# Hash-bucketed attention kernel: one flag matmul per block, one normalisation per head, V's scale matmul ahead of the scores, bits in two steps

## Chip, core and metric

The kernel runs on one core of a Trainium2 chip. The metric is the device time of one execution in microseconds (us); three executions of the kernel before took 687.52, 689.46 and 691.98 us, so its time is 689.46 us (median). A core has a matrix engine (TensorE, PE; its weight loads are listed apart as PEld), VectorE (DVE), ScalarE (ACT), GpSimd (POOL) and a queue engine (SP) that issues most of the DMAs here.

## What is computed

Attention in which a query sees only the keys of its own hash bucket, then two dense layers. Shapes: batch 2, 8 heads, 768 positions, head size 64.

```python
q_bits = (einsum('bhsd,dk->bhsk', q, proj) > 0)          # 6 bits, k_bits the same way
mask = q_bucket[:, :, :, None] == k_bucket[:, :, None, :]
scores = where(mask, (1 / sqrt(D)) * q @ k.T, -1e9)
scores = scores - max(scores, axis=-1)
attn = exp(scores); attn = attn / (sum(attn) + 1e-9)
x = attn @ v                                              # then to (1536, 512)
h = maximum(maximum(x @ w1, x @ w2), x @ w3); x = h @ w_out
h = x @ w_in; return (h * clip(h + 3, 0, 6) / 6) @ w_out2
```

A query whose bucket holds no key has all scores at -1e9 and so gets the mean row of V.

## The kernel before

**Steps.** The 16 heads (8 pairs `p`, two heads `j` each; `h = 2p + j`) are cut into 96 score units, six for each head: two halves `hf` of 384 queries, three units of 256 keys each. A loop runs over steps `s` = 0 to 101 (`NST + LAG`). Step `s` writes out, in this order on TensorE: the block product `pv` of block `s - 6` (`LAG` is 6), the step's tasks, `scores` of unit `s`, and the row maxima `max_unit` of a later head (10 units ahead). Every engine runs its instructions in the order in which this loop writes them. The instructions that split an exponential (`psplit`) follow, then the tasks that are named in `AFTER` or come before step 8, and then the late tasks.

**One step on TensorE.** `scores` makes four matmuls of 384 columns (line 664): two of Q by K in high and low parts (`QB`, `KB`), two over rows of `T` tiles that hold the high parts, the hash bits and the row maxima. ScalarE reads the result `s` twice: exponential `E` in fp32 (line 668), and `ph`, the same in fp16 (line 671, one unit in twelve on VectorE). GpSimd subtracts (`pl`, line 686). `max_unit` makes two matmuls (line 614), which VectorE reduces (line 618). `pv` handles one block of 128 queries, three to a half, once all three units of that half are there: 6 key tiles times three matmuls of 65 columns (lines 698 to 700: `ph` by V's high and low half, `pl` by the high half; column 65 sums the weights), then two matmuls for the queries without a key: `FL` (one row of flags) by V's mean row in `VM`, its high half (line 703) and its low half (line 704). Each of these twenty loads its own weights.

**PSUM.** There are three pools: `s`, 2 buffers of two banks; `x`, one bank; `m`, three banks (maxima, bits, transposes, V's mean and scale). The three blocks of a half add into one `x` tile at columns 0, 66 and 132. `norm` (lines 710, 715, 718, on VectorE) reads it at the end of the half: denominator `xd`, reciprocal `xr`, product `xo`. As there is one `x` buffer, the first block of the next half waits for `xo`. It is written in steps with `s % 6` of 2 and 5, right behind the block.

**Other work that the change touches.** `vsum` (line 543) is one matmul with `ones` that spreads the pair's maximum of |V|, from which V's scale is made; it is named in `AFTER` and so is written behind the maxima of its step (`s % 12 == 6`). `bits` computes hash signs of a half pair: six matmuls (line 147) and one compare on VectorE (line 513); both halves stand in one step (`BT`, 13 steps ahead of the pair). `max_out` sends the two maximum rows (`T<-mr`) and the flags (`FL<-mf`, line 651) by DMA on SP's queue, two steps ahead of the head. `vmean` (line 596) sums V by matmuls whose result is the same on every partition, and makes `VM` from partition 0.

**After the loop** come the two dense layers: matmuls of 384 and 512 columns with three products each.

Of the kernel before, what the change touches and what calls it, by code (L numbers as in the profile page):

```python
# [24 lines left out]
VW = 130  # L25
# [7 lines left out]
RAMP = 8  # L33
AFTER = ("vmean", "vsum")
WARM = (9, 4, 3, 1)
# [18 lines left out]
AK, AQ = -15, -16  # L54
BT = (-13, -13)
BO = (-12, -11)
# [48 lines left out]
def body(ctx, tc, qT, kT, vP, projT, wts, consts, out):  # L105
# [251 lines left out]
    def attention():  # L357
# [5 lines left out]
        VV = [ap.tile([128, KT, 2, VW], F16, name=f"VV{i}") for i in range(2)]  # L363
        VM = [ap.tile([128, 2, VW], F16, name=f"VM{i}") for i in range(2)]
        FL = [ap.tile([128, S], F16, name=f"FL{i}") for i in range(3)]
# [224 lines left out]
        def vmean(p):  # L590
            u = unit()
            w = VV[p % 2]
            o = u[:, 0:130].rearrange("p (j d) -> p j d", j=2)
            for kt in range(KT):
                for c in (0, 65):
                    pe.matmul(
                        o, one16, w[:, kt, :, c:c + 65], start=kt + c == 0,
                        stop=kt == KT - 1 and c > 0,
                    )
            m = ap.tile([1, 2, 64], F32, name="vm_m")  # L600
            act.activation(out=m, in_=o[0:1, :, 0:64], func=AF.Copy, scale=1.0 / S)
            vm = VM[p % 2][0:1]
            eng = pool if p else dve
            eng.tensor_copy(out=vm[:, :, 0:64], in_=m)
            eng.tensor_tensor(out=vm[:, :, 65:129], in0=m, in1=vm[:, :, 0:64], op=ALU.subtract)

# [39 lines left out]
        def max_out(h, q=None, eng=None):  # L646
            r, g = st.pop(("mr", h, q))
            c = slice(0, S) if q is None else hsl(q)
            for i in range(2):
                copy(QA[h % NA][96 + i:97 + i, c], r[:, i, :], eng)  # L650
            (eng or sp).dma_start(out=FL[h % 3][0:1, c], in_=g)

# [36 lines left out]
        def pv(h, hf, q):  # L689
            p, j = divmod(h, 2)  # L690
            if q == 0:
                st["X", h, hf] = unit("x")
            o = st["X", h, hf][:, 66 * q:66 * q + 65]
            for kt in range(KT):
# [6 lines left out]
            c = slice(hf * HF + 128 * q, hf * HF + 128 * q + 128)  # L701
            f, vm = FL[h % 3][:, c], VM[p % 2][:, j, :]
            pe.matmul(o, f, vm[:, 0:65], start=False, stop=False)
            pe.matmul(o, f, vm[:, 65:130], start=False, stop=True)

        def norm(h, hf):
            p, j = divmod(h, 2)
            X = st.pop(("X", h, hf))[:, 0:198].rearrange("p (b d) -> p b d", b=3)
            d = a2.tile([128, 3], F32, name="xd")
            dve.tensor_scalar(  # L710
                out=d, in0=X[:, :, 64], scalar1=1e-9, scalar2=up[:, p:p + 1],
                op0=ALU.add, op1=ALU.mult,
            )
            r = a2.tile([128, 3], F32, name="xr")
            dve.reciprocal(out=r, in_=d)
            if j == 0 and hf == 0:
                st["xo", p] = a2.tile([128, 6, 128], F32, name="xo")
            dve.tensor_tensor(  # L718
                out=st["xo", p][:, 3 * hf:3 * hf + 3, 64 * j:64 * j + 64], in0=X[:, :, 0:64],
                in1=r.unsqueeze(2).to_broadcast([128, 3, 64]), op=ALU.mult,  # L720
            )
# [9 lines left out]
        def at(s, fn, *a):  # L731
            tasks.setdefault(s, []).append((fn, a))
# [54 lines left out]
        for p in range(NP):  # L787
# [36 lines left out]
            for j in range(2):  # L824
                h = 2 * p + j
                if h:
                    at(s0 + 6 * j + MF, max_fin, h)
                    at(s0 + 6 * j + MO, max_out, h)
                for hf in range(2):
                    at(s0 + 6 * j + 3 * hf + 2 + LAG, norm, h, hf)  # L830
            for hf in range(2):
# [24 lines left out]
        for s in range(NST + LAG):  # L856
            if 0 <= s - LAG < NST:
                pv(*idx(s - LAG))
# [9 lines left out]
            for g in gs:  # L868
                next(g, None)
            if 0 <= s - 1 < NST:  # L870
                psplit(*idx(s - 1), gs)
# [794 lines left out]
```

## Time and profile before

| | |
|---|---|
| three executions | 687.52, 689.46, 691.98 us |
| profiled execution | 693.22 us, of it span 691.4 us |
| PE busy | 668.5 us (97%) |
| PEld busy | 613.1 us (89%) |
| DVE, ACT, POOL busy | 507.7 (73%), 432.1 (63%), 330.8 (48%) us |
| mean granted clock of TensorE | 0.993 |

The attention loop fills the span up to about 250 us. A busy PE is not a full one: the profile lets each matmul last until its result is out, about 0.19 us for 65 columns, while the next starts 0.03 us later. What a matmul costs in a row of others is the distance from its start to the next one's start. A wait is idle time of an engine that a named instruction ended. The granted clock is 1.00 at TensorE's upper level (2.4 GHz) and 0.5 at its lower (1.2 GHz).

### The profile page before, as it was taken

Reading aid. Unit: us, or ns where it says so; the run is one execution under the profiler, and the core shown is the slowest. Engines: PE = TensorE matmul, PEld = TensorE weight load, DVE = VectorE, ACT = ScalarE, POOL = GpSimd, SP = SyncE. Lnnn points to the kernel's source line nnn. Section 1 sums busy time; section 2 is a strip of 40 time slices with the busy share of each in tenths; the row PEclk is TensorE's granted clock in tenths of the full one; section 3 lists DMA queues with packets and bytes.
Section 4 is the critical chain, followed back from the end, with each engine's and each line's share of the span. In section 5 each row is a group of like instructions: output and inputs, shape, how many; then the busy total and the mean of one; then the engine's idle time right before and its main releaser. Section 6 shows DMA issues by size and latency. Waiting matters only on the chain. (4 is left out here: it accounts for less than half of the span.)

```text
span 691.4 us, 13485 instructions
## 1 busy us (share of the span) xinstructions
PE 668.5 (97%) x5189; PEld 613.1 (89%) x5189; DVE 507.7 (73%) x978; ACT 432.1 (63%) x749; POOL 330.8 (48%) x280
## 2 busy tenths in 40 slices
PE   8999999999999999999999999899999999999998
PEld 7789898888898989999998899878898898898986
DVE  6888987999985547677667347974768687877664
ACT  7658787898888525574745456686656565665530
POOL 6778888899988240655441242313142331313100
PEclk9999999999999999999999999999999999999999
DMA  6655656667441000211121320022213030211004
GB/s 190 169 155 133 168 140 156 173 165 195 107 97 63 2 1 32 90 64 62 62 92 34 120 92 31 31 74 79 86 36 122 21 102 31 92 60 63 1 0 183
DMA packets 22527, 61.80 MB, mean 89 GB/s; under 512 B 3864, under 2 KB 4952, under 8 KB 22464
## 3 DMA queue, kind: packets, MB, share of 16 engines
q1 hardware_dynamic: 22032, 60.55, 30.7%
q8 instruction: 41, 0.67, 0.4%
q10 hardware_dynamic: 432, 0.40, 0.2%
q14 instruction: 22, 0.18, 0.1%
HBM read 38.87 MB, written 3.15 MB: 61 GB/s over the span
## 5 line engine op out<-in xcount | busy, mean ns | idle before, releaser
L686 POOL TENSOR_TENSOR pl<-E,ph 128x768 f16<-128x768 f32 x85 | 152.5, 1809 | 30.8 <-ACT ph L671 18.1
L618 DVE TENSOR_REDUCE mx<-m 128x1 f32<-128x384 f32 x192 | 96.7, 546 | 13.9 <-PE m L614 13.0
L668 ACT ACTIVATE E<-s 128x768 f32<-128x768 f32 x96 | 78.0, 813 | 40.7 <-PE s L664 32.9
L671 ACT ACTIVATE ph<-s 128x768 f16<-128x768 f32 x85 | 68.9, 811 | 0.0
L698 PEld LDWEIGHTS <-ph 128*128 128x128 f16 x576 | 54.3, 98 | 16.5 <-issue 10.5
L698 PE MATMUL x<-VV,ph 128*128 128x65 f16 x576 | 65.2, 196 | 2.7 <-DVE xo L718 1.9
L699 PE MATMUL x<-VV,ph 128*128 128x65 f16 x576 | 64.7, 197 | 0.0
L700 PE MATMUL x<-VV,pl 128*128 128x65 f16 x576 | 64.2, 194 | 0.0
L614 PE MATMUL m<-T,T 76*128 76x384 f32 x192 | 54.4, 354 | 3.5 <-DVE mx L618 1.5
L664 PE MATMUL s<-QB,KB 128*128 128x384 f32 x192 | 57.1, 379 | 0.4 <-ACT ph L671 0.4
L699 PEld LDWEIGHTS <-ph 128*128 128x128 f16 x576 | 54.8, 99 | 0.6 <-issue 0.6
L700 PEld LDWEIGHTS <-pl 128*128 128x128 f16 x576 | 55.1, 100 | 0.0
L664 PE MATMUL s<-T,T 98*128 98x384 f32 x192 | 50.0, 342 | 0.9 <-DMA T<-mr 0.8
L983 POOL TENSOR_TENSOR wl<-wy,wh 128x512 fp32r<-128x512 f32 x11 | 14.3, 1304 | 75.6 <-ACT wh L981 75.6
L1005 POOL TENSOR_TENSOR hF<-hF 128x256 f32<-128x256 f32 x8 | 6.3, 785 | 89.3 <-DVE hF L964 89.3
L614 PEld LDWEIGHTS m<-T,T 76*128 76x128 f32 x192 | 35.3, 190 | 9.4 <-DVE mx L618 5.7
L960 DVE SCALAR_TENSOR_TENSOR wy<-wy,wr 128x512 int32<-128x512 int32 x32 | 22.8, 713 | 26.6 <-ACT wr L955 26.6
L1547 DVE TENSOR_TENSOR xF<-x,xF 128x512 f32<-128x512 f32 (+1 forms) x43 | 29.4, 684 | 11.8 <-PE x L1529 11.7
L1088 POOL TENSOR_TENSOR hF<-hF 128x256 f32<-128x256 f32 x6 | 6.6, 1093 | 62.7 <-DVE hF L1047 62.7
L664 PEld LDWEIGHTS s<-T,T 98*128 98x128 f32 x192 | 35.3, 191 | 1.5 <-DMA T<-mr 1.5
L1547 DVE TENSOR_TENSOR xF<-m,xF 128x512 f32<-128x512 f32 (+1 forms) x42 | 28.5, 678 | 4.6 <-PE m L1529 4.6
L1246 ACT ACTIVATE gr<-m,half 128x384 f32<-128x384 f32 x30 | 17.3, 577 | 21.5 <-DVE m L1224 13.0
(470 smaller groups left out, 2169.0 us busy)
## 6 DMA issues: line engine op xcount, KB each, us to landing
wraw<-in_wts_dram SPq DMA_DIRECT2D x56, 512.0 KB
xF<-in_vP_dram SPq DMA_DIRECT2D x8, 384.0 KB
KB<-kH SPq DMA_DIRECT2D x15, 192.0 KB
QB<-qL SPq DMA_DIRECT2D x15, 192.0 KB
T<-kH SPq DMA_DIRECT2D x15, 192.0 KB
T<-qH SPq DMA_DIRECT2D x15, 192.0 KB
KB<-kL SPq DMA_DIRECT2D x15, 192.0 KB
QB<-qH SPq DMA_DIRECT2D x15, 192.0 KB
```

What stands on the lines that cost most here:

```text
L614: pe.matmul(u[:, 0:HF], QA[h % NA][0:76, qt * 128:qt * 128 + 128], KA[h % NA][0:76, hsl(hf)], start=True, stop=True,)
L618: dve.tensor_reduce(out=mx[h][:, qt, hf:hf + 1], in_=u[:, 0:HF], axis=AX.X, op=ALU.max)
L664: pe.matmul(u[:, k, 0:HF], a[0:n, c], b[0:n, hsl(hf)], start=n == 128, stop=n < 128)
L668: act.activation(out=e, in_=u[:, :, 0:HF], func=AF.Exp, scale=BIG)
L671: act.activation(out=ph.rearrange("p (a b) -> p a b", a=2), in_=u[:, :, 0:HF], func=AF.Exp, scale=BIG,)
L686: eng.tensor_tensor(out=pl, in0=e, in1=ph, op=ALU.subtract)
L698: pe.matmul(o, ph[:, c], vv[:, 0:65], start=kt == 0, stop=False)
L699: pe.matmul(o, ph[:, c], vv[:, 65:130], start=False, stop=False)
L700: pe.matmul(o, pl[:, c], vv[:, 0:65], start=False, stop=False)
L960: dve.scalar_tensor_tensor(out=y0, in0=y0, scalar=3, in1=r3, op0=ALU.logical_shift_left, op1=ALU.bitwise_or)
L1246: act.activation(out=r, in_=u, func=AF.Relu, bias=half, scale=1.0 / 6.0)
L1547: dve.tensor_tensor(out=o, in0=u[:, 0:c1 - c0], in1=o, op=ALU.add)
```

## The change

- **Flags.** The flags are sent twice, to rows 0 and 32 of `FL`; `VM` holds the mean's high half in row 0 and its low half in row 32, with zeros between. One matmul per block does what two did. `vmean` works on 33 partitions in place of 1.
- **Normalisation.** All six blocks of a head add into one `x` bank, at columns 0, 66, ... 330, and one `norm` per head reads it, in the step with `s % 6 == 5`.
- **Place of the first block.** In the step with `s % 6 == 0`, in which a head's first block comes, `pv` is written behind the scores and the maxima instead of ahead of everything.
- **V's scale.** `vsum` leaves `AFTER`, and so stands ahead of the scores.
- **Bits.** The first half's bits move one step forward (`BT` is (-14, -13)).

```diff
-AFTER = ("vmean", "vsum")
+AFTER = ("vmean",)
-BT = (-13, -13)
+BT = (-14, -13)
...
-        VM = [ap.tile([128, 2, VW], F16, name=f"VM{i}") for i in range(2)]
+        VM = [ap.tile([128, 2, 65], F16, name=f"VM{i}") for i in range(2)]
...
-            m = ap.tile([1, 2, 64], F32, name="vm_m")
-            act.activation(out=m, in_=o[0:1, :, 0:64], func=AF.Copy, scale=1.0 / S)
-            vm = VM[p % 2][0:1]
+            m = ap.tile([33, 2, 64], F32, name="vm_m")
+            act.activation(out=m, in_=o[0:33, :, 0:64], func=AF.Copy, scale=1.0 / S)
+            vm = VM[p % 2][0:33, :, 0:64]
             eng = pool if p else dve
-            eng.tensor_copy(out=vm[:, :, 0:64], in_=m)
-            eng.tensor_tensor(out=vm[:, :, 65:129], in0=m, in1=vm[:, :, 0:64], op=ALU.subtract)
+            eng.tensor_copy(out=vm, in_=m)
+            eng.tensor_tensor(out=vm[32:33], in0=m[32:33], in1=vm[32:33], op=ALU.subtract)
...
-            (eng or sp).dma_start(out=FL[h % 3][0:1, c], in_=g)
+            for r in (0, 32):
+                (eng or sp).dma_start(out=FL[h % 3][r:r + 1, c], in_=g)
...
-            if q == 0:
-                st["X", h, hf] = unit("x")
-            o = st["X", h, hf][:, 66 * q:66 * q + 65]
+            if hf == q == 0:
+                st["X", h] = unit("x")
+            o = st["X", h][:, 66 * (3 * hf + q):66 * (3 * hf + q) + 65]
...
-            f, vm = FL[h % 3][:, c], VM[p % 2][:, j, :]
-            pe.matmul(o, f, vm[:, 0:65], start=False, stop=False)
-            pe.matmul(o, f, vm[:, 65:130], start=False, stop=True)
-
-        def norm(h, hf):
+            pe.matmul(o, FL[h % 3][:, c], VM[p % 2][:, j, :], start=False, stop=True)
+
+        def norm(h):
             p, j = divmod(h, 2)
-            X = st.pop(("X", h, hf))[:, 0:198].rearrange("p (b d) -> p b d", b=3)
-            d = a2.tile([128, 3], F32, name="xd")
+            X = st.pop(("X", h))[:, 0:396].rearrange("p (b d) -> p b d", b=6)
+            d = a2.tile([128, 6], F32, name="xd")
...
-                for hf in range(2):
-                    at(s0 + 6 * j + 3 * hf + 2 + LAG, norm, h, hf)
+                at(s0 + 6 * j + 5 + LAG, norm, h)
...
-            if 0 <= s - LAG < NST:
+            after = (s - LAG) % 6 == 0 and 0 <= s < NST
+            if 0 <= s - LAG < NST and not after:
                 pv(*idx(s - LAG))
...
             for g in gs:
                 next(g, None)
+            if after and s >= LAG:
+                pv(*idx(s - LAG))
```

On TensorE, at the start of the fourth head (step 18, whose scores are `s<-T_94,T_89`), the kernel before has the flags' two matmuls, the scores and maxima, then V's scale matmul, and then the next block (`LDWEIGHTS` rows are weight loads; `m` and `s` are PSUM tiles):

```order
L703 LDWEIGHTS FL_139
L703 MATMUL x<-VM_136,FL_139 128x65
L704 LDWEIGHTS FL_139
L704 MATMUL x<-VM_136,FL_139 128x65
L664 MATMUL s<-QB,KB 128x384 x2
L664 MATMUL s<-T_94,T_89 128x384 x2
L614 MATMUL m<-T_90,T_95 128x384 x2
L543 MATMUL m<-vs_s,ones 128x1
L698 LDWEIGHTS ph
```

The same place of the changed kernel, from the last flag matmul of the head before (`FL_138`) on:

```order
L703 LDWEIGHTS FL_138
L703 MATMUL x<-VM_135,FL_138 128x65
L665 MATMUL s<-QB,KB 128x384 x2
L665 MATMUL s<-T_93,T_88 128x384 x2
L614 MATMUL m<-T_90,T_95 128x384 x2
L543 MATMUL m<-vs_s,ones 128x1
L665 MATMUL s<-QB,KB 128x384 x2
L665 MATMUL s<-T_94,T_89 128x384 x2
L614 MATMUL m<-T_90,T_95 128x384 x2
L699 LDWEIGHTS ph
```

One flag matmul and its weight load are gone; V's scale matmul stands ahead of step 18's scores; two steps' scores and maxima follow one another, and the head's first block comes behind both.

On VectorE, around one pair's bits (names: `mx` maxima, `pl` low part of the exponential, `bt` compare of the bits, `up` V's scale), before:

```order
L686 TENSOR_TENSOR pl<-E,ph 128x768
L618 TENSOR_REDUCE mx<-m 128x1 x2
L562 TENSOR_SCALAR up<-vs_r 128x1
L710 TENSOR_SCALAR xd<-x,up 128x3
L715 RECIPROCAL xr<-xd 128x3
L718 TENSOR_TENSOR xo<-x,xr 128x3x64
L513 TENSOR_SCALAR bt<-m,pr 128x384 x2
L618 TENSOR_REDUCE mx<-m 128x1 x2
```

and now:

```order
L687 TENSOR_TENSOR pl<-E,ph 128x768
L513 TENSOR_SCALAR bt<-m,pr 128x384
L618 TENSOR_REDUCE mx<-m 128x1 x2
L562 TENSOR_SCALAR up<-vs_r 128x1
L709 TENSOR_SCALAR xd<-x,up 128x6
L714 RECIPROCAL xr<-xd 128x6
L717 TENSOR_TENSOR xo<-x,xr 128x6x64
L513 TENSOR_SCALAR bt<-m,pr 128x384
L618 TENSOR_REDUCE mx<-m 128x1 x2
```

The normalisation covers six blocks here, the one three steps earlier is gone, and one of the two compares moved a step forward. On SP's queue every `FL<-mf` issue became two in a row, behind the maximum rows; behind the attention loop the order is the same on all engines.

## Rows read from the trace of the kernel before

**Rows 1.** Windows: length, busy us of each engine (instructions), granted clock, DMA share, GB/s.

```profile
150.00:180.00 30.00, 29.08 (x397) 25.89 (x396) 28.16 (x67) 27.10 (x42) 27.99 (x18) 1.00 0.68 174
...
262.00:691.40 429.40, 417.69 (x2185) 387.29 (x2184) 298.40 (x487) 239.16 (x471) 131.14 (x135) 1.00 0.21 67
```

**Rows 2.** Waits, TensorE matmuls, 35 to 250 us: us in total, times, longest.

```profile
PE x L698 <- DVE xo L718: 1.9, 3, 1.5
```

**Rows 3.** Waits, weight loads (PEld), 35 to 250 us.

```profile
PEld L698 <- issue: 10.5, 65, 0.3
PEld L698 <- DVE xo L718: 5.2, 10, 1.8
PEld m L543 <- DVE mx L618: 2.4, 3, 0.8
```

**Rows 4.** Timeline, TensorE: start, us, engine, line, instruction; end of a block, scores, next block.

```profile
148.62 0.19 PE L703 MATMUL x<-VM,FL 128*128 128x65 f16 x1
148.65 0.20 PE L704 MATMUL x<-VM,FL 128*128 128x65 f16 x1
...
148.96 0.59 PE L664 MATMUL s<-QB,KB 128*128 128x384 f32 x2
149.39 0.52 PE L664 MATMUL s<-T,T 98*128 98x384 f32 x2
...
150.36 0.19 PE L698 MATMUL x<-VV,ph 128*128 128x65 f16 x1
```

**Rows 5.** Timeline, VectorE: end of the normalisation between those two blocks.

```profile
149.95 0.36 DVE L718 TENSOR_TENSOR xo<-x,xr 128x192 f32<-128x192 f32 x1
```

**Rows 6.** Lines, VectorE, 35 to 250 us: form, count, busy us, mean ns, idle before.

```profile
L718 DVE TENSOR_TENSOR xo<-x,xr 128x192 f32<-128x192 f32 x32 | 11.4, 357 | 1.5
...
L710 DVE TENSOR_SCALAR xd<-x,up 128x3 f32<-128x3 f32 x32 | 6.7, 209 | 8.3 <-PE x L704 8.2
...
L715 DVE RECIPROCAL xr<-xd 128x3 f32<-128x3 f32 x32 | 5.6, 176 | 1.1
...
L314 DVE TENSOR_TENSOR hF<-m,hF 128x384 f32<-128x384 f32 x4 | 2.2, 552 | 2.8 <-PE m L307 2.8
```

**Rows 7.** Source, line 703: weight loads, ns min/median/max, first and last start.

```profile
L703 PEld LDWEIGHTS <-FL x96: 95/96/133, 35.5 to 248.0; 128*128 128x128 f16 x96
```

**Rows 8.** Timeline, TensorE, around V's scale matmul (line 543).

```profile
145.04 0.52 PE L614 MATMUL m<-T,T 76*128 76x384 f32 x2
146.03 0.38 PE L543 MATMUL m<-vs_s,ones 128*128 128x1 f32 x2 [0.47 <-DVE mx L618]
```

**Rows 9.** Timeline, TensorE: scores that follow a 384-column matmul of the bits.

```profile
157.01 0.51 PE L664 MATMUL s<-QB,KB 128*128 128x384 f32 x2
157.36 0.52 PE L664 MATMUL s<-T,T 98*128 98x384 f32 x2
```

**Rows 10.** Waits, ScalarE, 35 to 250 us.

```profile
ACT E L668 <- PE s L664: 26.5, 52, 2.3
```

**Rows 11.** Timeline: ScalarE's last read of scores 64, TensorE's first matmul of scores 66.

```profile
168.79 0.80 ACT L671 ACTIVATE ph<-s 128x768 f16<-128x768 f32 x1
...
171.19 0.42 PE L664 MATMUL s<-QB,KB 128*128 128x384 f32 x1
```

**Rows 12.** Source, line 651: the flags' DMA issues on SP's queue, ns.

```profile
L651 SPq DMA_DIRECT2D FL<-mf x17: 657/690/696, 17.0 to 218.0; - x17
```

**Rows 13.** Timelines, SP and TensorE: maximum rows issued, scores that read them; two heads.

```profile
112.05 1.75 SPq L142 DMA_DIRECT2D T<-mr  x2
...
116.44 0.59 PE L664 MATMUL s<-T,T 98*128 98x384 f32 x2 [0.76 <-DMA T<-mr]
...
139.63 0.77 SPq L142 DMA_DIRECT2D T<-mr  x1
...
144.69 0.52 PE L664 MATMUL s<-T,T 98*128 98x384 f32 x2
```

**Rows 14.** Window as in group 1, at a fall of the granted clock.

```profile
115.00:120.00 5.00, 3.76 (x40) 3.15 (x37) 4.00 (x10) 3.82 (x6) 3.30 (x3) 0.85 0.75 161
```

More of the change, by code (lines that the diff above doesn't have):

```diff
@@ L713, in norm @@
             )
-            r = a2.tile([128, 3], F32, name="xr")
+            r = a2.tile([128, 6], F32, name="xr")
             dve.reciprocal(out=r, in_=d)
-            if j == 0 and hf == 0:
+            if j == 0:
                 st["xo", p] = a2.tile([128, 6, 128], F32, name="xo")
             dve.tensor_tensor(
-                out=st["xo", p][:, 3 * hf:3 * hf + 3, 64 * j:64 * j + 64], in0=X[:, :, 0:64],
-                in1=r.unsqueeze(2).to_broadcast([128, 3, 64]), op=ALU.mult,
+                out=st["xo", p][:, :, 64 * j:64 * j + 64], in0=X[:, :, 0:64],
+                in1=r.unsqueeze(2).to_broadcast([128, 6, 64]), op=ALU.mult,
             )
```

## The prediction

> **What bounds the kernel now.** I read the windows first. In a window from the middle of the attention loop, 150 to 180 us, TensorE is busy for 29.08 of 30 us, and VectorE, ScalarE and GpSimd are close behind with 28.16, 27.10 and 27.99 [rows 1]. Behind the loop, from 262 us on, TensorE has 417.69 of 429.40 us and the others far less; no instruction changes its place there, so I carry those 429 us over as they are. All that can change lies in the first 250 us.
>
> Then the distances between starts, since a busy PE is not a full one. The second flag matmul starts at 148.65, 0.03 us behind the first at 148.62 [rows 4], so in a row of others it is worth 0.03 us. Matmuls of 384 columns are worth 0.35 / 2 = 0.175 us each: the two that start at 157.01 give way to the next pair at 157.36 [rows 9]. A step is then 20 x 0.03 + 4 x 0.175 + 2 x 0.175, about 1.65 us, plus its part of the bits, means and transposes; the flag matmuls of 96 steps start between 35.5 and 248.0 us [rows 7], 2.2 us a step. TensorE therefore streams for most of the loop; what remains are short waits. That is why I count TensorE's terms in full and those of the other engines only where TensorE waits for them.
>
> Then the waits. Two of them stand in the path of this change: the first block of a half waits for `xo` of the half before it, seen three times in the matmuls, 1.9 us [rows 2], and ten times in the weight loads, 5.2 us [rows 3]; and V's scale matmul waits for a reduction, three times, 2.4 us in the weight loads [rows 3]. ScalarE in turn idles 26.5 us for the scores [rows 10]: it is starved by TensorE, not the other way round. So a shorter TensorE sequence should show in the end.
>
> **The change part by part.**
>
> *One flag matmul per block.* It removes 96 matmuls with their weight loads. 96 x 0.03 = 2.9 us, on the path, since nothing else is issued in that gap.
>
> A weight load lasts 96 ns [rows 7], three times the distance between two pairs, so loads overlap with one another and with matmuls. The Trainium skill ("TensorE: Matmul & The Clock Gate", section "LDWEIGHTS (loading the stationary operand)") gives a load of P columns P / 1.2 ns, 107 ns for 128, which as a price for each removed pair would make this an estimate of 10.2 us and not 2.9. The trace agrees with the duration, not with its use as a price: 0.03 us start to start decides.
>
> *One normalisation per head.* Before, each of 32 halves costs VectorE 209 + 176 + 357 ns = 0.74 us [rows 6], 1.48 us a head. For six blocks I take the first two as they are (3 or 6 elements) and the last from another VectorE operation that reads PSUM with 384 elements, 552 ns [rows 6]: 0.94 us. VectorE saves 0.55 us for each of 16 heads, 8.7 us in all. VectorE isn't the engine that ends the loop; I count it at nothing by itself and keep it for the lower end of the range.
>
> What counts is the wait. The example: `xo` ends at 149.95 + 0.36 = 150.31 [rows 5], and the next block starts at 150.36 [rows 4], right behind it. There is no such hand-over inside a head any more. Between two heads the block now stands behind another set of scores and maxima, 6 x 0.175 = 1.05 us later, which covers the 0.94 us of the normalisation even where VectorE comes a little late. So all 13 waits go. Of their 1.9 + 5.2 = 7.1 us a part isn't lost time: the first load of a block idles 10.5 / 65 = 0.16 us even without a wait, while the maxima still stream [rows 3]. 7.1 - 13 x 0.16 = 5.0 us.
>
> *The moved first block.* In 15 steps the scores follow a matmul of 384 columns in place of one of 65. Behind narrow ones the two first matmuls of the scores take 149.39 - 148.96 = 0.43 us [rows 4], behind wide ones 0.35 [rows 9]: the heavier weight load has more to hide behind. 0.08 us for the 8 of those steps without V's scale matmul between: 0.6 us. It also brings the scores forward by a block, 20 x 0.03 = 0.6 us, and three things must be there by then. The buffer `s`: ScalarE's last read of scores 64 ends at 168.79 + 0.80 = 169.59, the scores that reuse it start at 171.19 [rows 11], after the change at 170.6 or so: 1.0 us to spare, no cost. The bank for the block itself: covered above. The maximum rows, by DMA: at the head where TensorE did wait for them, issue to use took 116.44 - 112.05 = 4.4 us; at the next it took 144.69 - 139.63 = 5.1 us without a wait [rows 13], so 0.7 us to spare, of which 0.6 go. I charge 1.0 us, for the one head that has waited (0.6) and some that come close; the ends are 0 and 15 x 0.6 = 9 us.
>
> *V's scale matmul.* Before, it is the third user of `m` in a row: the maxima start at 145.04 and stream for 0.35 us, to 145.39; it starts at 146.03 [rows 8]. 0.64 us, three times: 1.9 us. Ahead of the scores its bank has been free since the step before, and what comes next, four score matmuls, needs no `m`. It then holds a bank until VectorE reads it behind the step's maxima, about as late as before. I take 1.9 us; the lower end is 0, if the next maxima wait instead.
>
> *Bits in two steps.* The same twelve matmuls, once more 2.1 us of TensorE. ScalarE starves less at a time, and one compare on VectorE moves off the pile. 0 us on the path, cover: TensorE streams the same columns either way.
>
> *What is added.* A second flag DMA per issue, 17 x 0.69 us = 11.7 us of SP's issue time [rows 12], behind the maximum rows of its own head and needed only six steps later; the loads behind it come 0.7 us later and are used several steps later. The means on 33 partitions: no row shows that form; ends are no change and, if it doubled, under half a us on GpSimd for each of eight pairs, hidden by four steps of lag. Zero.
>
> *The other engines.* A faster TensorE meets GpSimd. Spread over 215 us, the gain of 2.9 + 5.0 + 1.9 + 0.6 = 10.4 us is 1.45 us of each 30; GpSimd has 30 - 27.99 = 2.0 us left in the fullest window [rows 1]. It fits, barely; I charge 1.0 us.
>
> **The sum**, against the profiled execution's 693.22 us: -2.9 - 5.0 - 0.6 - 1.9 + 1.0 + 1.0 = -8.4, so 684.8 us. That execution is 3.8 us above the median of the three, 689.46; the same step from the median gives 681.1, and I say 681 us.
>
> **Rivals.**
>
> *The waits only move.* The time that `xo` no longer takes is taken by the next thing: a maximum's bank that VectorE hasn't freed, or an exponential that ScalarE can't start since GpSimd holds `E`. For it: all four engines stand at 90% or more [rows 1]. Against: ScalarE's 26.5 us of idle time for the scores [rows 10], and VectorE's relief. Then only the flags and the narrow hand-over remain, 3.5 us: 686 us.
>
> *Slower: the maximum rows come late.* Scores of a new head now want them 0.6 us sooner, and 0.7 us are to spare. Each further 0.1 us of lateness costs 15 x 0.1 = 1.5 us. If SP's additional issue, 0.69 us [rows 12], came to stand ahead of the rows at every head, 15 x 0.6 = 9 us would eat the gain; at 1.1 us of lateness it is 15 x 1.0 = 15 us against 9.4, 695 us. From 0.7 us on it decides. Against: in the order the second flag DMA stands behind the rows, and two steps lie between their issue and the scores.
>
> *The clock.* Around 118 us the granted clock fell: 0.85 over 115 to 120 us, with TensorE busy only 3.76 of 5 us there, just behind the wait for the maximum rows at 116.44 [rows 13, 14]. At the lower of the two levels (a half) each matmul takes twice as long; a mean of 0.85 loses 15% of 5 us, 0.75 us, in that window, and the next one may lose as much again. Fewer waits may leave such falls out, with 1.5 to 3.5 us more gained: 678 us. Or the wait for the rows grows and the fall stays.
>
> *The load as price.* If a removed pair were worth its load's 96 ns [rows 7], 9.2 us would go for 2.9: 675 us. The Trainium skill's rule on weight loads, above, would have it so. The distance of starts speaks against it.
>
> **How the numbers follow.** Chances: forecast 0.50, waits only move 0.33, clock 0.10, load as price 0.02, maximum rows late 0.05. The forecast's gain runs from 6 to 11 us, since the charges and the 1.9 us are uncertain. About 1% (7 us, so under 682.6 us) is what a measurement of this kernel can tell from no change. Of the forecast 0.08 lies above that. Faster by over 1%: 0.42 + 0.10 + 0.02 = 0.54. Within 1%: 0.33 + 0.08 = 0.41. Slower: 0.05. The range, 675 to 688 us, takes in the clock and nearly all of the second case; late rows and the far ends stay out.
>
> **What would show it.** Waits of line 699 (the block's first matmul) for `xo`: none left. V's scale matmul: no wait for a reduction. Sixteen `xo` of about 0.55 us. Flag matmuls: 96, still 0.03 us to the next. The loop's end some 8 us earlier and the stretch behind it as long as before, 429 us. Wrong, if scores wait for `T<-mr` or for ScalarE more than a few us in all, if the maxima (line 614) wait more than before, or if GpSimd stands at 97% and ScalarE waits for `pl`.

## The result, and the profile after

The changed kernel takes **695.22 us** (median; 691.65 to 697.8), the kernel before on the same chips 689.25 (687.41 to 691.98): ratio 1.008, 95% interval 1.0062 to 1.0097. It is 6 us slower, where 8 us less were forecast. The profiled execution took 693.62 us, of it span 691.8. (The profiled execution of the kernel before, 693.22 us, was slower than all 11 executions of this comparison, so the two spans say little; medians and single stretches are compared below.) One execution of all those below, 702.16 us of a_bits_back, ran in a slower state of the chip and is left out.

| | before | after |
|---|---|---|
| median | 689.25 us | 695.22 us |
| PE busy | 668.5 us | 664.2 us |
| DVE busy | 507.7 us | 503.1 us |
| granted clock, mean of executions | 0.9959 (138, those run beside the experiments) | 0.9926 (11) |

Work did leave the kernel: TensorE and VectorE are each busy for over 4 us less. The windows (length, then busy us and count for PE, PEld, DVE, ACT, POOL, then granted clock, DMA share, GB/s) show that TensorE, VectorE, ScalarE and GpSimd all wait more in the loop, answering [rows 1]:

```profile
15.00:35.00 20.00, 19.11 (x83) 16.32 (x82) 14.86 (x39) 10.24 (x13) 10.86 (x7) 0.74 0.64 169
...
150.00:180.00 30.00, 27.60 (x361) 24.70 (x360) 25.75 (x56) 24.80 (x38) 25.64 (x17) 0.99 0.61 160
262.00:691.80 429.80, 418.45 (x2200) 387.97 (x2198) 299.27 (x488) 241.06 (x473) 131.22 (x135) 1.00 0.21 67
```

In 150 to 180 us TensorE is busy for 27.60 us (29.08 before) with 361 matmuls in place of 397, and no other engine took its place: VectorE, ScalarE and GpSimd fell from 27 or 28 us to between 24.8 and 25.8. From 262 us on things stand as they were. So the loss is in the loop and, with a granted clock of 0.74 from 15 to 35 us, in the opening.

The flag matmuls, which mark the loop, start between 40.4 and 249.7 us here. In a second profile of the kernel before, g_before below, they start between 35.7 and 244.9 us. In these two executions the loop itself takes the same time, 209.3 and 209.2 us: what the change was to gain there went into new waits and a fall of the clock (0.95 from 120 to 150 us). The rest of the difference stands ahead of the loop, about 1 us of it because the first block now follows its step's scores and maxima. The clock differs from one execution to the next, though, so it is the experiments, and not these two profiles, that divide the loss among the parts.

The waits of TensorE's matmuls, 35 to 250 us (us in total, times, longest), answering [rows 2]:

```profile
PE m L147 <- DVE mf L643: 5.3, 6, 1.2
PE m L614 <- DVE mx L618: 3.3, 7, 0.7
PE m L543 <- DVE mx L618: 1.4, 2, 0.9
PE m L543 <- DMA FL<-mf: 1.0, 1, 1.0
```

No wait for `xo` is left, as predicted. In its place stand the bits (L147), which wait six times for `mf` and did not wait at all before; the maxima (L614), which waited 0.3 us for `mx` before; and V's scale matmul (L543), which was to wait no more. Every name ahead of an arrow is an `m` tile: all of these are waits for one of the three `m` banks of PSUM. ScalarE, which waited 26.5 us for the scores [rows 10], now waits longer:

```profile
ACT E L669 <- PE s L665: 40.2, 51, 3.2
```

Two stretches of the timeline show the mechanism (start, us, engine, line, instruction, wait). First, bits ahead of the scores, TensorE and VectorE at 71 to 74 us:

```profile
71.21 0.27 PE L634 MATMUL m<-ident,mq 128*6 128x128 f32 x1
...
71.58 1.09 DVE L682 CAST ph<-E 128x768 f16<-128x768 f32 x1
...
72.58 0.94 DVE L466 SCALAR_TENSOR_TENSOR qL<-qr,qH 128x768 fp32r<-128x768 f32 x1
...
73.97 0.27 DVE L643 TENSOR_SCALAR mf<-m 6x128 f16<-6x128 f32 x1
...
74.38 0.41 PE L147 MATMUL m<-kH,prH 128*128 128x384 f32 x1 [1.23 <-DVE mf L643]
```

Line 634 transposes a head's maxima into an `m` bank. That bank is free only when `mf`, the last of three reads by VectorE, is done, and VectorE comes to it behind two long operations, at 73.97 + 0.27 = 74.24. The step's two maxima take the other two banks, and a user of `m` written ahead of the next scores is the third: it gets the transpose's bank again. The matmul queue is in order, so the scores behind the bits wait too. While the bits stood a step later, this bank was needed only behind four score matmuls.

Second, the moved block and V's scale, 143 to 149 us:

```profile
143.50 0.54 PE L614 MATMUL m<-T,T 76*128 76x384 f32 x2
...
143.93 0.56 DVE L717 TENSOR_TENSOR xo<-x,xr 128x384 f32<-128x384 f32 x1
144.40 1.01 DVE L618 TENSOR_REDUCE mx<-m 128x1 f32<-128x384 f32 x2
145.00 0.38 PE L543 MATMUL m<-vs_s,ones 128*128 128x1 f32 x2 [0.97 <-DMA FL<-mf]
145.18 0.63 ACT L193 ACTIVATE m<-wraw 128x512 f32<-128x512 f32 x1
...
146.03 0.33 PE L614 MATMUL m<-T,T 76*128 76x384 f32 x1
146.40 0.56 DVE L618 TENSOR_REDUCE mx<-m 128x1 f32<-128x384 f32 x1 [0.99 <-PE m L614]
147.01 0.55 PE L614 MATMUL m<-T,T 76*128 76x384 f32 x1 [0.65 <-DVE mx L618]
...
148.07 0.15 DVE L549 TENSOR_SCALAR vs_t<-m 128x1 f32<-128x1 f32 x1
...
148.52 0.68 DVE L217 SCALAR_TENSOR_TENSOR m<-m,wr 128x512 int32<-128x512 int32 x1
```

V's scale at 145.00 stands right behind the maxima of 143.50, as it did before, since the block between them moved away. It waits for the first of their reductions, which VectorE starts at 144.40, behind the normalisation. (The row names the flags' DMA, which had long landed.) Then it keeps its bank until VectorE reads it at 148.07, behind the step's reductions. Another bank is with the dense layers' weight preparation, from ScalarE's `m<-wraw` at 145.18 to VectorE's read at 148.52. That leaves one bank for both maxima of the step: the second starts at 147.01, right after the reduction of the first ends at 146.40 + 0.56 = 146.96. Right behind this stretch, in which TensorE was busy for 1.68 us of the 3.30 from 144.0 to 147.3, the granted clock was at its lower level (0.50, 1.2 GHz) for 3 us:

```profile
147.30:150.30 3.00, 3.00 (x42) 2.94 (x42) 2.22 (x6) 0.50 (x1) 2.85 (x2) 0.50 0.48 100
```

### The profile page after: what moved, and what is told of

It reads as the page before. It is cut to its first block, busy times and chain, and to the rows that moved or that the text cites. A ratio compares the mean times of both kernels' runs of the same rounds, so it can differ in the third digit from the quotient of the medians.

```text
span 691.8 us, 13313 instructions
## 1 busy us (share of the span) xinstructions
PE 664.2 (96%) x5093; PEld 611.2 (88%) x5093; DVE 503.1 (73%) x930; ACT 430.9 (62%) x749; POOL 329.9 (48%) x280
## 5 line engine op out<-in xcount | busy, mean ns | idle before, releaser
L699 PE MATMUL x<-VV,ph 128*128 128x65 f16 x576 | 64.2, 196 | 0.0
L700 PE MATMUL x<-VV,ph 128*128 128x65 f16 x576 | 63.7, 197 | 0.0
L614 PE MATMUL m<-T,T 76*128 76x384 f32 x192 | 55.7, 362 | 5.3 <-DVE mx L618 4.4
L614 PEld LDWEIGHTS m<-T,T 76*128 76x128 f32 x192 | 35.8, 193 | 12.0 <-DVE mx L618 10.2
L665 PEld LDWEIGHTS s<-QB,KB 128*128 128x128 f32 x192 | 31.2, 196 | 0.0
```

The lines of the kernel that those rows point to most:

```text
L614: pe.matmul(u[:, 0:HF], QA[h % NA][0:76, qt * 128:qt * 128 + 128], KA[h % NA][0:76, hsl(hf)], start=True, stop=True,)
L665: pe.matmul(u[:, k, 0:HF], a[0:n, c], b[0:n, hsl(hf)], start=n == 128, stop=n < 128)
L699: pe.matmul(o, ph[:, c], vv[:, 0:65], start=kt == 0, stop=False)
L700: pe.matmul(o, ph[:, c], vv[:, 65:130], start=False, stop=False)
```

## The experiments

All kernels compute the whole reference. "before" is the kernel before on the same chip. A part, such as **bits**, is that part of the change as the diff above has it.

### One part at a time

Each is the kernel before with one part only.

```diff
 b_bits_alone        BT = (-14, -13)
 f_vsum_alone        AFTER = ("vmean",)
 c_flags_alone       VM, vmean, max_out (two DMAs), one flag matmul
 d_norm_alone        one x bank and norm(h) per head, first block behind the maxima
```

> The kernel before with only the bits' first half a step earlier (BT (-14, -13)). Theory 1, the bank: about 1 us of wait at each of six pairs, 694 to 695 us, and waits of the bits for line 643. If moving the bits only spreads work, 689 us or a little less.

> The kernel before with only V's scale matmul ahead of the scores. Here a block product stands between the maxima of the step before and the scale matmul, so VectorE has about 0.6 us to free a bank. Theory 4: the three waits of 0.64 us go, 687.5 to 689 us. If the scale matmul ahead of the scores costs by itself: 692 us or more.

> The kernel before with only the one flag matmul per block, its doubled DMA and the means on 33 partitions. From the distance of starts, 96 x 0.03 us = 2.9 us less than before: 686.5 us. Theory 2, the clock: if the doubled DMAs thin out TensorE's work in the opening, the granted clock falls there and the time is 692 us or more.

> The kernel before with only one normalisation per head, one bank, and the head's first block behind the scores and maxima. From the waits for xo, 13 x 0.39 us = 5.0 us less, and 0.6 us for the hand-over: 684 us. Theory 3, the moved block starves something: 689 us or more, with new waits of the scores or the maxima that add up to 5 us.

| only | median | ratio to before (95%) | worked out |
|---|---|---|---|
| bits | 692.40 | 1.0042 (1.0028 to 1.0056) | +2.9 us |
| V's scale | 691.82 | 1.0037 (1.0016 to 1.0058) | +2.5 us |
| flags | 689.90 | 1.0007 (0.9989 to 1.0025) | +0.5 us |
| normalisation and place | 689.83 | 1.0000 (0.9984 to 1.0016) | 0 |

(Ratio less 1, times 689.3 us.) The sum is 5.9 us; the whole loss, worked out in the same way from 1.008, is 5.5 us. Each part is known to 1 to 1.5 us only, so that the two agree so well is partly luck. The mean granted clock of bits and V's scale alone, 0.9954 each, is that of before within 0.0005, so it is not the clock that makes these two slower. Two parts cost time and the two from which the gain was to come gain nothing. The kernel before, run once more under another label, gave 0.9989 (0.9971 to 1.0007).

> The kernel before once more, for a second profile: its first one, 693.22 us, is above all its other executions. Expected: 688 to 691 us, and a loop (first block product to last flag matmul) that is 1 to 3 us shorter than the first profile's 213.1 us, without the 1.9 us of wait for the maximum rows at 116 us.

Its median is 688.36 us, and in its profile the loop, first block product to last flag matmul, takes 209.8 us, without the wait at 116 us.

For the normalisation the weight loads' waits, 35 to 250 us, show what came in the place of `xo`. First the kernel before (g_before), then d_norm_alone:

```profile
PEld L698 <- DVE xo L718: 4.9, 9, 1.8
PEld m L614 <- DVE mx L618: 2.9, 8, 0.6
PEld m L614 <- DVE mf L643: 1.8, 4, 1.1
PEld s L664 <- DMA T<-mr: 0.4, 1, 0.4
```

```profile
PEld m L614 <- DVE mx L618: 5.0, 15, 0.6
PEld m L614 <- DVE mf L643: 3.1, 6, 1.2
PEld s L664 <- DMA T<-mr: 2.5, 4, 1.2
```

These rows are 10.0 us before and 10.6 us with the part: the wait for `xo` is gone to the last, and maxima and scores wait instead. (Such idle times overlap with matmuls that still stream, so they rank waits and don't add up to lost time. All listed waits of the matmuls themselves in this window are 5.7 us before and 4.9 with the part.) Two steps' maxima follow one another now; that VectorE's reductions, half a us each with the normalisation among them, then free three banks too slowly is one explanation, and l_norm_between below tests it.

### Parts taken back, and two remedies that cost more

```diff
 a_bits_back = after,        BT = (-13, -13)
 e_bits_vsum_back = a,       AFTER = ("vmean", "vsum")
 h_fin_early = after,        MF, MO = -4, -2      # transpose a step earlier
```

> The changed kernel with both halves' bits in one step again (BT back to (-13, -13)). Theory 1, the bank: in the changed kernel the first half's bits stand three m-uses behind the transpose of the maxima, whose bank VectorE frees only with the flags' compare (line 643); the trace of the changed kernel shows about 1.0 us of wait at each of six pairs, so this kernel should be about 6 us faster than the changed one, near 689 us, and the waits of line 147 for line 643 should be gone. Theory 2, the clock: what costs is the granted clock at the lower level in the opening (10 us of it in the profiled run of the changed kernel); then this kernel stays within 2 us of the changed one, 693 to 697 us. Theory 3, the moved block starves something: no change either, and the time stays near 694 us with a granted clock near 1.00.

> The changed kernel with the bits in one step and V's scale matmul behind the maxima again: what is left is the one flag matmul and the one normalisation. Each of the two alone left the time where it was (689.9 and 689.8 against 689.5 us), while both together with V's scale matmul ahead cost 4 us (693.7). Theory 4, the collision: with the first block moved, the scale matmul stands right behind the step before's maxima and ahead of the scores, waits there for a bank and holds up the scores; then this kernel is near 689.5 us or under, 4 us below the one with the scale matmul ahead. Theory 5, flags and normalisation disturb one another: 692 us or more.

> The changed kernel with the transpose of the maxima one step earlier (MF -4), so that two more pairs of maxima stand between it and the first half's bits and the bank that the bits take is another one. Theory 1, the bank: the waits of the bits for line 643 (6.3 us in the changed kernel) fall below 1 us, and the time by 2 to 5 us from 695 us, unless the transpose then waits for the maxima's last reduction. If the bits wait for something else (their operands), the wait stays.

With the bits back 693.46 us (1.0052, 1.0032 to 1.0073), with V's scale back as well 691.07 (1.0022, 1.0002 to 1.0041). From 1.008 these are steps of 1.9 and 2.1 us, less than the 2.9 and 2.5 of the parts alone but within the intervals. So flags and normalisation together are not a gain but some 1.5 us of loss. With the transpose a step earlier 700.99 us (1.0164, 1.0141 to 1.0187), the worst of all: the bits find their bank, but the transpose itself now comes before the reduction that it reads is done, as the waits of h_fin_early's matmuls show:

```profile
PE m L634 <- DVE mq L625: 8.2, 13, 1.4
```

### Is it the bank?

If the held bank is the cause, the part must become harmless when its `m` user is moved to where the bank costs nothing, with all its work kept. Each of these is the kernel before with one edit.

```diff
 k_bits_behind: first half's bits in step -14, written behind that step's scores and maxima
+AFTER = ("vmean", "vsum", "bits0")
 n_vsum_read: V's scale ahead of the scores, and VectorE's read of it ahead of the reductions
+at(s0 + VS, vscale, p, 0)          # vs_t; was po(...), behind psplit
 l_norm_between: normalisation per head, first block behind the scores, ahead of the maxima
```

> The kernel before with the first half's bits a step earlier, but behind that step's scores and maxima instead of ahead of them, so that the transpose's bank has been freed. Theory 1, the bank: the wait that cost 2.9 us ahead of the scores (4.6 us of waits of the bits) is gone; 688.5 to 690 us. If it is the splitting of the bits that costs, whatever the bank, 692 us as with the bits ahead.

> The kernel before with V's scale matmul ahead of the scores, as in the version that cost 2.3 us, but with VectorE's first read of its bank (line 549) moved ahead of the step's reductions, so that the bank is held for a short time only. Theory 4 in its sharper form, the bank is held across the step's maxima: the 1.9 us of waits of the scale matmul are gone and the maxima's waits don't grow; 687.5 to 689.5 us. If the scale matmul ahead of the scores costs by itself, 691.5 us or more.

> The kernel before with one normalisation per head and the head's first block behind the scores but ahead of the maxima. Theory 8, the maxima of two steps in a row overrun the three banks: in the version with the block behind the maxima, waits of the maxima grew by 3 us, which took back what the normalisation gave. Here they should stand at the 4.3 us of before (max after max 2.7, max after scores 1.5), the blocks should wait for xo by 0.2 to 0.4 us at each of 15 heads, and the time be 687 to 689 us. If the gain fell to something else, 689.5 us or more.

Bits behind: 690.81 us, 1.0006 (0.999 to 1.0021) against 1.0042 ahead. The row of b_bits_alone's matmuls that goes with the cost has no counterpart in k_bits_behind, whose matmuls of L147 wait for nothing between 35 and 250 us (their weight loads 1.7 us, for `mx`):

```profile
PE m L147 <- DVE mf L643: 3.6, 6, 0.9
```

This move also frees the scores from standing behind six matmuls of the bits. That alone is worth nothing here: k_bits_behind is no faster than the kernel before, in which all twelve stand ahead of the scores.

V's scale with its read moved: 689.09 us, 0.9982 (0.9964 to 0.9999) against 1.0037. In f_vsum_alone, where a block still stands ahead of V's scale, its matmul has no wait left, as forecast; the maxima behind it wait instead. With the read moved they are back at the 0.3 us of before. First f_vsum_alone, then n_vsum_read:

```profile
PE m L614 <- DVE mx L618: 2.3, 4, 0.7
```

```profile
PE m L614 <- DVE mx L618: 0.3, 1, 0.3
```

Both costs are gone with the same instructions run, and the waits that went with them, so for these two the held bank is shown, not only argued.

The block between scores and maxima: 690.08 us, 0.9998 (0.9982 to 1.0014), no gain either, though a block stands between the two steps' maxima there. So that the banks take back what the normalisation was to give is not shown. Behind the last flag matmul the normalisation loses something too: 13 us of windows from there, first g_before, then l_norm_between:

```profile
244.90:257.90 13.00, 13.00 (x86) 12.90 (x83) 2.49 (x7) 3.43 (x7) 1.28 (x1) 1.00 0.01 1
```

```profile
245.90:258.90 13.00, 12.62 (x82) 12.19 (x79) 4.52 (x8) 2.73 (x6) 3.19 (x2) 1.00 0.01 1
```

TensorE gets 82 matmuls through and not 86, and from the last flag matmul to the end of the span it is 686.5 - 244.9 = 441.6 us in the one and 688.9 - 245.9 = 443.0 in the other; 442.1 in the changed kernel.

### What the second flag DMA costs

```diff
 j_dma_alone = before, but
-(eng or sp).dma_start(out=FL[h % 3][0:1, c], in_=g)
+for r in (0, 32):
+    (eng or sp).dma_start(out=FL[h % 3][r:r + 1, c], in_=g)
 r_flags_late = before + flags, but the two DMAs in a task of their own, behind the next rows
+po(s0 + 6 * j + 2, flag_out, h)    # four steps behind the maximum rows, four ahead of use
 q_flags_read = before + flags + n_vsum_read
 t_late_read  = r_flags_late + n_vsum_read
```

> The kernel before with only the flags sent twice (rows 0 and 32; the matmuls read the second row against zeros), the two flag matmuls kept. The one flag matmul with the doubled DMA left the time at 689.9 us where 2.9 us less were expected. Theory 6, the DMAs cost what the matmuls give: 691 to 692.5 us here, and a lower granted clock in the opening. Theory 7, the matmuls' time is taken back by the waits for the banks of the maxima: no change here, 689 to 690 us.

> The kernel before with one flag matmul per block, and the flags' two DMAs issued behind the next rows instead of directly behind the maximum rows (one to five steps later, still ahead of the block that reads them). Theory, the second flag DMA costs time because SP's queue has no gap in the opening and everything behind it starts 0.7 us later for each (the third pair's rows were issued at 28.23 us in place of 26.71 with the doubled DMA): with the DMAs out of the way the cost of 1.6 us goes and the flag matmuls give what the rest of the loop lets through, 1 to 1.5 us: 688 us, ratio 0.998. Rival, the doubled DMAs cost by their traffic or the flags give nothing: 689.5 to 690 us as with the flags alone, ratio 1.001.

> The kernel before with one flag matmul per block, and V's scale matmul ahead of the scores with its sum read ahead of the reductions; normalisation and bits as before. Theory: the two are independent, the flags give no more than their two DMAs cost (+0.5 us alone), V's scale gives 1.2 us: about 688.5 us, ratio 0.999. Rival, the flags' matmuls do shorten the loop where the maxima no longer wait for the bank of V's scale: 2.9 - 1.6 + 1.2 = 2.5 us, 687 us, ratio 0.996.

> The same as r_flags_late, and V's scale matmul ahead of the scores with its sum read ahead of the reductions. Theory: the gains add, 688 - 1.2 = 687 us, ratio 0.997. Rival, the same interplay as in q_flags_read, where the two together were 3 us slower than before though each alone was not: 691 us or more, ratio 1.004.

| | median | ratio to before (95%) | mean granted clock |
|---|---|---|---|
| second DMA alone (j) | 691.13 | 1.0025 (1.0004 to 1.0046) | 0.9938 |
| flags, DMAs at once (c) | 689.90 | 1.0007 (0.9989 to 1.0025) | 0.9942 |
| flags, DMAs later (r) | **687.37** | 0.9969 (0.9947 to 0.9991) | 0.9976 |
| q, DMAs at once | 692.10 | 1.0047 (1.0031 to 1.0064) | 0.9938 |
| t, DMAs later | 688.47 | 0.9978 (0.9957 to 0.9999) | 0.9959 |

The DMA whose cost was set at nothing costs 1.7 us (0.3 to 3.2 by the interval). With both out of the way the flags gain 2.1 us, and q and t, which differ in that and a third buffer for `mf`, are 0.0069 apart, 4.8 us. So whether the flags gain hangs on the place of these DMAs in the queue.

By which wait it costs time is open. Over the opening, first g_before, then j_dma_alone, the two profiles differ in the granted clock:

```profile
15.00:35.00 20.00, 18.42 (x111) 15.16 (x110) 17.40 (x42) 12.55 (x17) 13.14 (x8) 1.00 0.68 185
```

```profile
15.00:35.00 20.00, 19.07 (x83) 16.26 (x82) 14.81 (x39) 10.24 (x13) 10.80 (x7) 0.74 0.63 167
```

No matmul of j_dma_alone waits for a DMA between 15 and 70 us (a weight load does once, for 0.3 us), though the queue runs 1.5 us late; its first flag matmul starts at 39.0 us in place of 35.7, and by the end 1.7 us of that are left. In q_flags_read, whose clock stood at 1.00 there, scores do wait, between 36 and 70 us, in two rows that t_late_read doesn't have:

```profile
PE s L665 <- ACT ph L672: 1.9, 1, 1.9
PE s L665 <- DMA T<-mr: 0.9, 1, 0.9
```

The mean clocks, 0.0021 lower in j than in before and in q than in t, are worth some 0.7 us each by the line given under "The clock" below, so less than half of either difference.

r_flags_late has the lowest median here. That t is no faster than r, though n_vsum_read alone was a little faster than before, was not looked into; the two intervals overlap.

### The changed kernel, mended

```diff
 o_mended = after + bits0 in AFTER + vs_t read ahead of the reductions
 u_all_mended = o_mended + the flags' DMAs four steps later
```

> The changed kernel with its two held banks mended: the first half's bits stay a step earlier but stand behind that step's scores and maxima, and VectorE reads V's scale sum ahead of the step's reductions. All else as changed (one flag matmul, one normalisation per head, moved first block, V's scale matmul ahead of the scores). Theory, held PSUM banks: the two edits give back what they gave back in the kernel before, 2.9 - 0.2 and 2.3 + 0.7 us, so 695.2 - 5 to 5.7 = 689.5 to 690 us, ratio 1.000 to 1.002 to the kernel before. Rival, the sum of many small waits and more falls of the clock with all five parts together: no more than 2 us come back, 693 us or more, ratio at least 1.005.

> The changed kernel with its held banks mended as in o_mended and the flags' DMAs issued behind the next rows. Theory, the queue in the opening is what o_mended still lost: 691.9 - 1.6 - some falls of the clock = 689 to 690 us, ratio 1.000 to 1.002. Rival, the rest of o_mended's loss is in the moved block and its waits for the maxima's banks: 691.5 to 692 us, ratio 1.003 to 1.004.

The same causes in the changed kernel itself: with both banks mended 691.88 us, 1.0034 (1.0009 to 1.0059); with the DMAs later as well **688.48 us, 0.9971 (0.9952 to 0.9991)**. From 0.8% slower the five parts come to 0.3% faster with nothing left out, only three things written at another place and a third buffer for `mf`. o_mended gave back 0.46% (3.2 us) where 5 to 5.7 were expected; the later DMAs gave another 0.63% (4.3 us), of which the higher mean clock, 0.9967 in place of 0.9926, makes some 1.4 by the same line. But r_flags_late, which has the flags alone, stands at 0.9969: the other parts, mended, add nothing to it. SP's queue in the opening, first o_mended, then u_all_mended:

```profile
24.03 1.62 SPq L142 DMA_DIRECT2D T<-bt  x2
...
27.32 1.36 SPq L655 DMA_DIRECT2D FL<-mf  x2
28.77 0.54 SPq L142 DMA_DIRECT2D KB<-kL  x1
...
34.92 1.52 SPq L142 DMA_DIRECT2D T<-mr  x2
```

```profile
23.94 1.56 SPq L142 DMA_DIRECT2D T<-bt  x2
...
27.16 0.54 SPq L142 DMA_DIRECT2D KB<-kL  x1
...
33.32 1.51 SPq L142 DMA_DIRECT2D T<-mr  x2
```

Both come to `T<-bt` at 24.0 us. With the flags in the row, the next pair's rows go out at 28.77 in place of 27.16 and the maximum rows at 34.92 in place of 33.32, 1.6 us later: between 24 and 40 us this queue has hardly a gap, and everything behind the flags moves. The Trainium skill ("DMA: Bandwidth & Descriptors", section "Rules for kernel authors") says of spreading DMAs over issuing engines that it saves only the sequencer's issue time. In this case the place of that time counted: the DMA engines stood at 0.64 of their time (window 15 to 35 us of the changed kernel), and the same DMAs at another place in the same queue gave the loss back.

## Why the prediction was wrong, point by point

The step that failed is the judgement that the moved bits would cost nothing and V's scale give 1.9 us, since no wait for a bank was seen on their new places: the two cost 5.4 us, each alone, and 4.0 us when they are taken out of the changed kernel. The gain that was to stand against them failed too: the waits for `xo` were set at 5.0 us and gave nothing, and the second flag DMA, set at nothing, took back what the flag matmuls gave.

**The bits, "0 us on the path, cover: TensorE streams the same columns either way".** This step failed most: +2.9 us. Columns were counted, banks were not. The moved bits became the third user of `m` behind the transpose, and waited for VectorE's `mf` six times, 5.3 us in all.

**V's scale, -1.9 us, "its bank has been free since the step before".** False from the order itself: with the block moved, V's scale follows the maxima of the step ahead directly, just as it followed those of its own step before. It still waits (1.4 + 1.0 us), and in addition holds its bank over the whole step. With the block left in its place (f_vsum_alone) it doesn't wait, and the held bank alone costs the time. "What comes next needs no `m`" looked four matmuls ahead; the maxima behind them need two. The lower end given, 0 "if the next maxima wait instead", was too mild: alone it is +2.5 us, and with the read moved ahead of the reductions -1.2 (0.0018 of 689; the interval reaches from -2.5 to -0.1).

**The waits for `xo`, -5.0 us.** That they would all go was right, and `xo` takes 558 ns for 384 elements, as predicted (about 0.55):

```profile
L717 DVE TENSOR_TENSOR xo<-x,xr 128x384 f32<-128x384 f32 x15 | 8.4, 558 | 0.5
```

But the gain is 0 (0.9984 to 1.0016), and the 5.0 us were too much from the start. The three waits of the matmuls are at the same blocks as three of the ten waits of the weight loads; two of the pairs, in the kernel before:

```profile
209.51 0.20 PE L698 MATMUL x<-VV,ph 128*128 128x65 f16 x1 [0.30 <-DVE xo L718]
243.93 0.20 PE L698 MATMUL x<-VV,ph 128*128 128x65 f16 x1 [1.47 <-DVE xo L718]
```

```profile
209.51 0.10 PEld L698 LDWEIGHTS <-ph 128*128 128x128 f16 x1 [0.62 <-DVE xo L718]
243.93 0.10 PEld L698 LDWEIGHTS <-ph 128*128 128x128 f16 x1 [1.79 <-DVE xo L718]
```

So ten blocks waited and not 13, and the sum of 7.1 us has three waits twice. 5.2 less 10 x 0.16 is 3.6 us at most, and the matmuls themselves stood still for 1.9 us, of which 1.47 at one block near the end of the loop. d_norm_alone's profile fits the smaller figure: its last flag matmul starts at 243.4 us, in g_before at 244.9, with a granted clock of 1.00 up to 250 us in both. The stretch behind the loop takes about as much back (below). The rest stays open.

The rival "the waits only move" named "a maximum's bank that VectorE hasn't freed", and it was given 0.33. Its price was wrong: it kept the 3.5 us of flags and hand-over and let the waits only come back in full. In fact the parts also made new ones, and so it gave 686 and no loss. No case of the prediction had the three `m` banks as the thing that decides, though its signs of being wrong had them: "if the maxima (line 614) wait more than before" came true, 3.3 us for `mx` against 0.3.

**The flags, -2.9 us.** Still 96 matmuls and loads of 96 ns:

```profile
L703 PEld LDWEIGHTS <-FL x96: 96/96/133, 40.4 to 249.7; 128*128 128x128 f16 x96
```

With equal DMAs they gain 0.18%, 1.2 us (c against j, whose intervals overlap); with the DMAs out of the row 2.1 us (r against before), which holds the gain from moving the row's first DMA too. So 2.9 was rather high, as far as these two tell, and the distance of starts the better price: the load's duration would have made it 9.2 us. What failed is the term beside it, "the loads behind it come 0.7 us later and are used several steps later". That was argued from the middle of the loop; in the opening the queue is full and the delays add up, whichever wait they end in: with the second DMA alone the third pair's first `KB` row goes out at 28.23 us, in g_before at 26.71.

**Hand-over, late maximum rows, GpSimd.** The hand-over's 0.6 us can't be told from the rest. The charge of 1.0 us for late rows was of the right kind: scores wait for `T<-mr` in d_norm_alone (2.5 us in the loads), but not in the changed kernel between 40 and 250 us. GpSimd never became the bound: 25.64 of 30 us.

**The stretch behind the loop, carried over as it was.** Nearly right: 442.1 to 443.0 us from the last flag matmul to the end in the five profiles with one normalisation per head and a granted clock of 1.00 from 300 to 420 us, 441.6 in g_before, so 0.5 to 1.4 us longer.

**The clock.** The rival had fewer falls; there were more. Over all executions here one whose mean granted clock is 0.0025 lower takes 0.88 us longer (a line through the executions of all kernels here, each kernel's mean taken off). The changed kernel's clock is 0.0033 below that of before: by this estimate 1.2 of the 6 us. It is lower in the kernels that send both flag DMAs at once (0.9922 to 0.9942, a_bits_back apart with 0.9954) and not in those that send them later (0.9959 to 0.9976). That the late queue brings falls on may be guessed from this, but no trace shows the step from one to the other. One trace speaks against it: f_vsum_alone, with one flag DMA, had the same fall from 17.5 to 21 us as j_dma_alone, a clock of 0.53 and 0.54. It stays open.

So the loss is: bits +2.9, V's scale +2.5, and two parts without a gain. One, the flags, was eaten by its own second DMA in SP's queue. The other, the normalisation, had less to gain than was counted, and where that went is shown only in part.

## What to carry to other kernels

Before an instruction is moved, write down for each PSUM buffer who used it last, who reads that user and behind what, and who is next in the ring: a move that leaves every engine's work the same can turn the third user of three banks into a wait for the slowest reader. Write an early user behind the urgent ones, or bring its read forward; that took away 0.36% and 0.55% here. And look at each queue where it is fullest, in the opening, not in the middle of the loop: a DMA of 0.7 us put ahead of other rows took back all that the matmuls saved. And when waits are added up, check that a matmul's wait and its weight load's are not the same one.

## What the hardware showed that was not expected

The number of falls of the granted clock differs from execution to execution of one kernel: mean clocks of 0.988 to 1.000 in the changed kernel, with 697.53 us at 0.988 and 691.65 at 1.000. What one costs can be read behind the loop, where the instructions are the same. First the profile before, then g_before, each from 60 us behind its last flag matmul:

```profile
308.10:408.10 100.00, 96.96 (x545) 95.46 (x544) 60.76 (x101) 53.17 (x110) 42.58 (x45) 0.98 0.24 79
```

```profile
304.90:404.90 100.00, 96.97 (x554) 95.47 (x553) 62.35 (x102) 53.16 (x110) 42.73 (x45) 1.00 0.22 79
```

From the last flag matmul to the end the one takes 443.3 us and the other 441.6; two more profiles of kernels with the old normalisation had such a fall between 300 and 420 us, 443.2 and 442.9 us, and seven more had none, 441.5 to 442.0. Where they fall differs as well: the opening of the changed kernel had a clock of 0.74 in the profiled execution above, that of the kernel before 1.00 in the same window. A single profiled execution can therefore be 4 us off its kernel's median, as that of the kernel before was; a sum made against it must be carried to the median, and a comparison of spans alone would have shown no loss here at all.
